# W_up loaded whole in pass 10 of the first loop, three chunks of W_down behind W_gate, and tile 1's attention result transposed by DMA

## The chip, the cores and the metric

The kernel runs on one core of a Trainium2 chip. A core has a matrix engine (TensorE, PE in the profile, with its weight loads as PEld), a vector engine (VectorE, DVE), an engine for activations (ScalarE, ACT), a general engine (GpSimd, POOL) and SyncE (SP), which here issues nearly all transfers. SBUF is the working memory, PSUM the accumulator memory that TensorE writes, with eight banks. The metric is the device time of one execution in microseconds; the median of three runs of the kernel before is 271.67 us, the lowest 271.39 and the highest 271.82.

## The reference

One transformer block on x of 2048 rows and 640 columns in bf16: linear attention with 32 heads of 20 columns, then a gated feed-forward part with 1536 hidden columns.

```python
def _A_ref(x, wqkv, w_phi, wo):
    qkv = (x @ wqkv).reshape(B, S, 3, H, Dh) ...     # q, k, v by head
    pq = einsum("bhsd,hdf->bhsf", q, w_phi)
    pk = einsum("bhsd,hdf->bhsf", k, w_phi)
    phi_q = concat([softmax(pq), softmax(-pq)])
    phi_k = concat([softmax(pk), softmax(-pk)])
    kv = einsum("bhsf,bhsd->bhfd", phi_k, v)
    z  = einsum("bhsf->bhf", phi_k)
    num = einsum("bhqf,bhfd->bhqd", phi_q, kv)
    den = einsum("bhqf,bhf->bhq", phi_q, z) + 1e-6
    return (num / den) ... @ wo

def _B_ref(x, w_gate, w_up, w_down):
    return (gelu(x @ w_gate) * (x @ w_up)) @ w_down

h = x + _A_ref(layernorm(x), wqkv, w_phi, wo)
out = h + _B_ref(layernorm(h), w_gate, w_up, w_down)
```

## The kernel before

The rows are cut into 16 tiles of 128 (t = 0 to 15) and four blocks of four tiles (b = 0 to 3). The order of all engines' work is written out by hand: the order of the calls is the order on each engine, and waits and slots follow from it.

**First part.** Weights of q and k are multiplied with w_phi in the kernel (`fold`, L232). The loop of L494 runs over the 16 tiles. Each pass makes k of one tile (`k_tile`, pk), normalizes its exponentials (`k_norm`), and v of a later tile (`v_mm`, pv); layer-normalized rows are transposed by DMA into LN1T (`ln_ap`, L286). In passes 7 to 10 the q weights are loaded transposed (`load_T`, L203). In pass 10 tile 1's rows are transposed into LN1T of block 0 (L529), in pass 13 those of tile 0 (L531). In pass 15 the first four groups of q columns are multiplied (`q_mm`, pq, L396), the second of them from block 0, and `kv_tile` sums the key-value products. Behind the first of these groups a copy on GpSimd into Wg (L513) holds back the load of W_gate; after the loop SyncE issues W_gate in two parts (L539) and two of five row chunks of W_up (L540).

**The stretch around the change (L856 to L912).** Here the remaining q groups alternate with the attention of tiles 0 and 1. For one tile t: `attn_a` multiplies phi_q with kv and z (ab) and copies it to SBUF; `attn_b`, `attn_b2`, `attn_b3` divide by the sums on VectorE and leave o (L687); then o is transposed into oT, by DMA (`transpose_to` at L167) or on TensorE with a copy by ScalarE (L164, L165); `attn_c` multiplies oT with W_o (po, L708) in two halves of 320 columns; `attn_d` adds the residual into x_sb (L717); `attn_ds` takes the statistics (L121, L125; the reciprocal root on GpSimd, L140); `attn_ln` normalizes (L156) and `attn_e` transposes by DMA into LN2T, which the gate and up matmuls read. For tile 0 the transpose of o is a DMA; for tile 1 it is done on TensorE, between the two halves of tile 0's `attn_c`. After tile 0's `attn_b3` SyncE issues the other three chunks of W_up (L555) and three of twelve chunks of W_down (L560); five more follow behind a copy on GpSimd (L907), the last four later.

Then `gate_first` and `gate_second` make the first gate and up products, of tile 0 and then of tile 1 (gu, L762), and `weave` interleaves the rest: gate and up of each block, the attention of the later tiles, and `down` (pd, L814), which reads W_down and stores the output.

**PSUM.** Up to this point, and until `split` (L567), PSUM is a pool of four slots of two banks each (`gtile`); pq, ab, po, tp and gu take them in turn, each waiting until the slot's last tile has been read. A slot number is not written in the code: it follows from the order in which slots come free. After `split` there are eight slots of one bank (`bank`).

Of the kernel before, what the change touches and what calls it, by code (L numbers as in the profile page):

```python
# [8 lines left out]
BF16 = mybir.dt.bfloat16  # L9
F32 = mybir.dt.float32  # L10
ALU = mybir.AluOpType
# [6 lines left out]
def kernel(  # L18
# [12 lines left out]
    nc = tc.nc  # L31
    P = 128
    S = 2048
    D = 640
# [5 lines left out]
    NC = D // P  # L40
    NF = FF // P
    EPS = 1e-5
    HD = D // 2

    H0 = [(P * c) // Dh for c in range(NC)]
    NH = [(P * c + P - 1) // Dh - H0[c] + 1 for c in range(NC)]
# [31 lines left out]
    const = ctx.enter_context(tc.tile_pool(name="const", bufs=1))  # L78
# [8 lines left out]
    Wo = const.tile([P, NC, D], BF16, name="Wo")  # L87
    Wg = const.tile([P, NC, FF], BF16, name="Wg")
    Wu = const.tile([P, NC, FF], BF16, name="Wu")
    KT = [const.tile([P, SL * 32], BF16, name=f"KT{s}") for s in range(2)]  # L90
    KV = [const.tile([P, SL, 32], BF16, name=f"KV{s}") for s in range(2)]
    row = const.tile([P, 3, 32], F32, name="row")
# [3 lines left out]
    Eq = [const.tile([P, len(g), 2, 512], BF16, name=f"Eq{j}") for j, g in enumerate(QG)]  # L96
# [14 lines left out]
    def gtile(name):  # L111
        return psG.tile([P, 2, 512], F32, name=name, tag="G")
# [46 lines left out]
    def transpose_to(dst, src, on_pe, on_dve=False):  # L159

        if on_pe:
            tp = psG.tile([P, 16, P], BF16, name="tp", tag="G")
            for c in range(NC):
                nc.tensor.transpose(tp[:, c, :], src[:, c * P:(c + 1) * P], ident)  # L164
            (nc.vector.tensor_copy if on_dve else nc.scalar.copy)(dst, tp[:, 0:NC, :])  # L165
        else:
            nc.sync.dma_start_transpose(dst, src)  # L167
# [326 lines left out]
    for t in range(NT):  # L494
        if t == T3:
            kvp = gtile("kvp")[:, 0, 0:2 * QF].rearrange("p (s f) -> p s f", s=2)
        late = t in (1, 2, 3, 4)
        if 0 < t < NT - 6 and not late:
            ln_ap(t + 6, on_act=True)
        k_tile(t)  # L500
        if t == 0:
            ln_ap(6)
            nc.sync.dma_start(x_sb[3][:, 0:2, :], x_v[:, 12:14, :])
        if t in FQ:
            fold(WqT, Wq2, True, [i for i, f in enumerate(FQ) if f == t])
# [12 lines left out]
        if late:  # L518
            ln_ap(t + 6, on_act=True)
        if t == 1:  # L520
            nc.sync.dma_start(x_sb[3][:, 2:4, :], x_v[:, 14:16, :])
        if 0 < t < NT - 3:
            v_ev(t + 3)
        for i in ST.get(t, ()):
            ln_st(i, i + 1)
        k_norm(t)
        load_T(WqT, 0, *[i for i, f in enumerate(LQ) if f == t])
        if t == 10:
            transpose_to(LN1T[0][:, :, P:2 * P], ln_a(1), False)  # L529
        if t == 13:  # L530
            ln_ap(0, on_act=True)  # L531
        if t == 8:
            for z in KT:
                nc.gpsimd.memset(z, 0.0)
        if t == 5:
            nc.sync.dma_start(Wo, wo_v)
    q = len(QT)
    for a, b in ((0, 2), (2, NC)):
        nc.sync.dma_start(Wg[:, a:b], wg_v[:, a:b])  # L539
    nc.sync.dma_start(Wu[:, 0:2], wu_v[:, 0:2])  # L540
    for t in range(13, NT):
        kv_tile(t)
    kv_mask()
# [3 lines left out]

    p2 = ctx.enter_context(tc.tile_pool(name="p2", bufs=1, reuse_waits="tile"))
    p2r = ctx.enter_context(tc.tile_pool(name="p2r", bufs=1, side="right", reuse_waits="tile"))
    Wd = p2r.tile([P, NF, D], BF16, name="Wd")  # L550
    wd_v = B_w_down.rearrange("(c p) n -> p c n", p=P)

    def load_up():

        nc.sync.dma_start(Wu[:, 2:NC], wu_v[:, 2:NC])  # L555

    def load_down(*fs):

        for f, n in fs:
            nc.sync.dma_start(Wd[:, f:f + n], wd_v[:, f:f + n])  # L560

    ABs = [p2r.tile([P, 2, H, KC], F32, name=f"AB{i}") for i in range(2)]
    ABs += [LN1F[:, i * 2 * H * KC:(i + 1) * 2 * H * KC].rearrange("p (s h f) -> p s h f", s=2, h=H) for i in range(2)]
    LN2T, st = {}, {}
# [114 lines left out]
    def attn_b3(t, on_pe=False):  # L679
        AB, w = st[t]  # L680
        tt = p2.tile([P, 2, D], BF16, name="tt", bufs=2)
        num = bass.AP(AB.tensor, AB.offset, [AB.ap[0], [H * KC + 1, 2], [KC, H], [1, Dh]])
        nc.vector.tensor_tensor(  # L683
            tt.rearrange("p s (h f) -> p s h f", f=Dh), num,
            w[:, :, :, None].to_broadcast([P, 2, H, Dh]), ALU.mult)
        o = p2.tile([P, D], BF16, name="o", bufs=2)
        nc.vector.tensor_tensor(o, tt[:, 0], tt[:, 1], ALU.add)  # L687
        st[t] = o
        if not on_pe:
            attn_t(t, False)  # L690

    def attn_t(t, on_pe=True):
        oT = p2.tile([P, NC, P], BF16, name="oT", bufs=3)
        transpose_to(oT, st[t], on_pe)
        st[t] = oT

    def attn_c(t, between=None):

        if psB:
            po = pos = [bank("po")[:, 0:HD] for u in range(2)]  # L700
        else:
            po = gtile("po")
            pos = [po[:, u, 0:HD] for u in range(2)]
        for u in range(2):
            if u and between:
                between()
            for c in range(NC):
                nc.tensor.matmul(pos[u], lhsT=st[t][:, c, :], rhs=Wo[:, c, u * HD:(u + 1) * HD],  # L708
                                 start=(c == 0), stop=(c == NC - 1))
        st[t] = po  # L710

    def attn_d(t, act=True):

        ht = x_sb[t // 4][:, t % 4, :]
        h2 = ht.rearrange("p (u f) -> p u f", u=2)
        if not act:
            nc.vector.tensor_tensor(h2, st[t][:, :, 0:HD], h2, ALU.add)  # L717
# [82 lines left out]
    def down(b, tl, u, cut, pair):  # L800

        if u == 0:
            st["y"] = p2.tile([P, D], BF16, name="y", bufs=4)
        y = st["y"]
        last = b == NB - 1 and tl == 3
        edges = [(0, cut), (cut, D)][u]
        if last and u == 1:
            edges = (cut, cut + 192, D)
        for f0, f1 in zip(edges, edges[1:]):
            pd, rest = bank("pd"), None  # L810
            for f in range(NF):
                if f == NF // 2 and pair is not None:
                    rest = attn_two(pair, pd)
                nc.tensor.matmul(pd[:, 0:f1 - f0], lhsT=st[b, "g", f][:, tl * P:(tl + 1) * P],  # L814
                                 rhs=Wd[:, f, f0:f1], start=(f == 0), stop=(f == NF - 1), skip_group_check=pair is not None)
            nc.vector.tensor_tensor(y[:, f0:f1], pd[:, 0:f1 - f0], x_sb[b][:, tl, f0:f1], ALU.add)  # L816
# [45 lines left out]
    attn_b(0, True)  # L862
    attn_b2(0, True)
    attn_b3(0)
    load_up()
    load_down((0, 3))
    attn_a(1, 0)
    q_exp(q + 1, (0,))
    q_mm(q + 2)
# [2 lines left out]
    q_mm(q + 3)  # L872
    attn_b(1, True)
    attn_b2(1, True)
    attn_b3(1, True)
    q_exp(q + 2, (1,))
    q_mm(q + 4, (0,), (0, 1))
    attn_c(0, lambda: attn_t(1))
    attn_d(0, False)
    q_exp(q + 3, (0,))  # L880
    q_mm(q + 4, (0,), (2, 3))
    attn_ds(0)
    attn_c(1)
    q_exp(q + 3, (1,))
    attn_d(1, False)
    q_mm(q + 4, (0,), (4,))
    q_mm(q + 4, (1,))
    q_exp(q + 4)

    def first():  # L890
# [1 line left out]
        attn_e(0, None)  # L892

    attn_ds(1, first)
    q_mm(q + 5)
    q_exp(q + 5)
    q_mm(q + 6)
    q_exp(q + 6)
# [8 lines left out]
    nc.gpsimd.tensor_copy(Wd[:, 3, 0:1], Eq[q + 8][:, 0, 1, 0:1])  # L907
    load_down((3, 5))
    attn_a(2, 2)
    for f in range(4):  # L910
# [56 lines left out]
```

## Time and profile before

The profiled execution took 271.45 us, with a span of 269.7 us from the first to the last instruction.

| | |
|---|---|
| median of three runs | 271.67 us |
| profiled execution, its span | 271.45 us, 269.7 us |
| VectorE busy | 173.4 us (64%) |
| ScalarE busy | 138.4 us (51%) |
| GpSimd busy | 101.4 us (38%) |
| mean DMA rate over the span | 83 GB/s |
| granted TensorE clock | 1.000 |

In the profile an arrow points from what is read to what is written (out<-in), L is a line of the kernel, and a time in brackets is idle time of the engine ahead of the row with what ended it. TensorE's matmuls overlap in its pipeline, so a matmul's recorded duration is longer than the distance to the next; the chain of work that ended last gives the distances. The start of a row in the chain is therefore a little later than the start of the same instruction in the timeline.

### The profile page before, as it was taken

How to read it: one execution, taken by the hardware profiler on the slowest of the kernel's cores; microseconds unless marked ns; L12 is line 12 of the kernel's file. 1: busy time of each engine (PE TensorE's matmuls, PEld its weight loads, DVE VectorE, ACT ScalarE, POOL GpSimd, SP SyncE). 2: the span in 40 equal slices, each digit the busy share in tenths (PEclk: the TensorE clock that was granted, in tenths of full speed). 3: DMA queues.
4: the chain of work that ended last, by engine and by line, in shares of the span. 5: the costliest groups of instructions: out<-in, count | busy, mean ns of one | idle time of the engine just before them, and what ended most of it. 6: DMA issues, size and time to landing. Idle time of an engine off the chain costs nothing.

```text
span 269.7 us, 7099 instructions
## 1 busy us (share of the span) xinstructions
PE 266.0 (99%) x2892; PEld 172.4 (64%) x2892; DVE 173.4 (64%) x346; ACT 138.4 (51%) x247; POOL 101.4 (38%) x239
## 2 busy tenths in 40 slices
PE   8999999999999999999999999999999999999995
PEld 7777777755456877788755555775555476444574
DVE  5899999995875858875566783568664322333322
ACT  5779997877789665245541456321544300322100
POOL 5448988796003235375211664014661100000000
PEclk9999999999999999999999999999999999999999
DMA  6996579214673443234201225203222101000011
GB/s 192 211 212 150 103 195 92 53 29 137 276 254 73 147 123 70 58 74 52 51 27 49 49 50 51 51 2 79 76 43 49 24 24 51 24 0 2 1 49 49
DMA packets 45952, 22.27 MB, mean 83 GB/s; under 512 B 38496, under 2 KB 43872, under 8 KB 45920
## 3 DMA queue, kind: packets, MB, share of 16 engines
q1 hardware_dynamic: 45264, 21.80, 33.9%
q8 instruction: 22, 0.36, 0.6%
q10 hardware_dynamic: 656, 0.03, 0.2%
q14 instruction: 10, 0.08, 0.1%
HBM read 10.18 MB, written 2.62 MB: 47 GB/s over the span
## 4 chain that ended last, share of the span: by engine, by line
PE 97%; DMA 2%; SPq 0%; DVE 0%; issue 0%
PE gu L762 39%; PE pd L814 20%; PE pq L396 8%; PE pk L296 8%; PE po L708 8%; PE pv L296 7%; PE kvp L374 2%; DMA Wv<-in_A_wqkv_dram 2%; PE pv L312 2%; PE ab L619 1%; PE wa L248 1%; PE ab L586 1%; PE tp L164 0%; SPq L193 0%; SPq L190 0%; SPq L189 0%
## 5 line engine op out<-in xcount | busy, mean ns | idle before, releaser
L795 ACT ACTIVATE g<-gu 128x512 bf16<-128x512 f32 (+1 forms) x56 | 28.9, 519 | 73.4 <-PE gu L762 73.3
L762 PE MATMUL gu<-LN2T,Wg 128*128 128x512 bf16 (+2 forms) x320 | 62.5, 326 | 0.0
L762 PE MATMUL gu<-LN2T,Wu 128*128 128x512 bf16 (+2 forms) x320 | 62.5, 326 | 0.0
L798 DVE TENSOR_TENSOR GT<-gu,g 128x512 bf16<-128x512 f32 (+1 forms) x56 | 32.7, 591 | 45.6 <-PE gu L762 38.8
L814 PE MATMUL pd<-Wd,GT 128*128 128x320 bf16 (+4 forms) x396 | 53.9, 296 | 0.0
L814 PEld LDWEIGHTS <-GT 128*128 128x128 bf16 x396 | 37.6, 98 | 14.5 <-DVE GT L798 0.2
L762 PEld LDWEIGHTS <-Wu 128*128 128x128 bf16 x320 | 30.0, 98 | 22.4
L762 PEld LDWEIGHTS <-Wg 128*128 128x128 bf16 x320 | 29.7, 98 | 21.1 <-issue 0.2
L296 PEld LDWEIGHTS <-LN1T 128*128 128x128 bf16 x290 | 27.9, 98 | 10.4
L355 POOL TENSOR_TENSOR E<-E,rs 128x640 bf16<-128x640 bf16 x25 | 31.7, 1296 | 4.4 <-DVE rs L351 1.7
L816 DVE TENSOR_TENSOR y<-pd,x_sb 128x320 bf16<-128x320 f32 (+4 forms) x33 | 15.8, 480 | 24.1 <-PE pd L814 24.1
L708 PE MATMUL po<-Wo,oT 128*128 128x320 bf16 x160 | 24.5, 299 | 0.0
L296 PE MATMUL pk<-Wk,LN1T 128*128 128x320 bf16 x160 | 24.4, 300 | 0.0
L347 DVE TENSOR_REDUCE sk<-E 128x64 f32<-128x1280 bf16 x16 | 22.9, 1431 | 0.0
L396 PE MATMUL pq<-LN1T,Wq 128*128 128x512 bf16 x100 | 22.8, 380 | 0.0
L401 ACT ACTIVATE Eq<-pq 128x1024 bf16<-128x1024 f32 (+1 forms) x26 | 19.9, 832 | 2.5 <-PE pq L396 2.4
L340 ACT ACTIVATE E<-pk 128x640 bf16<-128x640 f32 x28 | 19.0, 766 | 3.0 <-PE pk L296 3.0
L708 PEld LDWEIGHTS <-oT 128*128 128x128 bf16 x160 | 15.6, 98 | 7.3 <-ACT oT L165 0.2
L296 PE MATMUL pv<-Wv,LN1T 128*128 128x320 bf16 x130 | 19.8, 300 | 0.0
L151 ACT ACTIVATE ln<-x_sb,v,rstd 128x640 bf16<-128x640 bf16 x14 | 12.9, 920 | 13.0 <-POOL v L747 12.8
L396 PEld LDWEIGHTS <-Wq 128*128 128x128 bf16 x100 | 9.5, 98 | 10.5
L683 DVE TENSOR_TENSOR tt<-AB,w 128x1280 bf16<-128x1280 f32 x10 | 15.1, 1507 | 1.0 <-POOL w L676 0.9
(122 smaller groups left out, 292.8 us busy)
## 6 DMA issues: line engine op xcount, KB each, us to landing
out_dram<-y SPq DMA_DIRECT2D x15, 160.0 KB, 1.9
x_sb<-in_A_x_dram SPq DMA_DIRECT2D x6, 320.0 KB, 3.5
Wg<-in_B_w_gate_dram SPq DMA_DIRECT2D x1, 1152.0 KB, 6.7
Wu<-in_B_w_up_dram SPq DMA_DIRECT2D x1, 1152.0 KB, 5.7
Wo<-in_A_wo_dram SPq DMA_DIRECT2D x1, 800.0 KB, 5.1
Wd<-in_B_w_down_dram SPq DMA_DIRECT2D x1, 800.0 KB
Wg<-in_B_w_gate_dram SPq DMA_DIRECT2D x1, 768.0 KB
Wu<-in_B_w_up_dram SPq DMA_DIRECT2D x1, 768.0 KB, 7.8
```

Source lines behind the costliest of these rows:

```text
L296: nc.tensor.matmul(ps[:, u, 0:HD], lhsT=lnT(t, c), rhs=W[:, c, u * HD:(u + 1) * HD], start=(c == 0), stop=(c == NC - 1))
L340: nc.scalar.activation(Ek[t][:, s, :].rearrange("p (u f) -> p u f", u=2), pk[:, :, 0:HD], ACTF.Exp, scale=((lnp[t][2], nrstd[t]) if t in C ...
L347: nc.vector.reduce_sum(sk, Ek[t].rearrange("p s (h f) -> p (s h) f", f=Dh), axis=AX.X)
L355: eng.tensor_tensor(e, e, rs[:, s * H:(s + 1) * H, None].to_broadcast([P, H, Dh]), ALU.mult)
L396: nc.tensor.matmul(pqs[j][:, i, :], lhsT=Wq2[:, kc, c * P:(c + 1) * P], rhs=LN1T[b][:, kc, :], start=(kc == 0), stop=(kc == NC - 1))
L401: nc.scalar.activation(Eq[j][:, :, s, :], pqs[j][:, 0:len(QG[j])], ACTF.Exp, scale=(1.0, -1.0)[s])
L708: nc.tensor.matmul(pos[u], lhsT=st[t][:, c, :], rhs=Wo[:, c, u * HD:(u + 1) * HD], start=(c == 0), stop=(c == NC - 1))
L762: nc.tensor.matmul(gu[i][:, 0:a1 - a0], lhsT=W[:, c, f * P:(f + 1) * P], rhs=LN2T[b][:, c, a0:a1], start=(c == 0), stop=(c == NC - 1))
L795: nc.scalar.activation(g[:, 0:n], gu[0][:, 0:n], ACTF.Gelu_apprx_tanh)
L798: nc.vector.tensor_tensor(st[b, "g", f][:, a0:a1], gu[1][:, 0:n], g[:, 0:n], ALU.mult)
L814: nc.tensor.matmul(pd[:, 0:f1 - f0], lhsT=st[b, "g", f][:, tl * P:(tl + 1) * P], rhs=Wd[:, f, f0:f1], start=(f == 0), stop=(f == NF - 1), ...
L816: nc.vector.tensor_tensor(y[:, f0:f1], pd[:, 0:f1 - f0], x_sb[b][:, tl, f0:f1], ALU.add)
```

## The change

W_up is loaded in one transfer of 1920 KB, issued by SyncE in pass 10 of the loop, behind the last part of the q weights and ahead of tile 1's transpose. Behind W_gate the first three chunks of W_down (480 KB) take the place of the two chunks of W_up; they have a tile of their own, Wd0, and the other nine chunks are in Wd1. The loads after tile 0's `attn_b3` are gone.

Tile 1's o is transposed by DMA like tile 0's. On TensorE the order becomes: both halves of tile 0's `attn_c`, the last three of five matmuls of q group 8, the first three of q group 9, `attn_c` of tile 1, the other two of group 9. Tile 1's residual is added in two halves of 320 columns. A tile of one slot of PSUM is taken by a memset of one element on VectorE, between tile 1's residual and its statistics.

```diff
+    ND = 3
+    Wd0 = const.tile([P, ND, D], BF16, name="Wd0")
...
         if t == 10:
+            nc.sync.dma_start(Wu, wu_v)
             transpose_to(LN1T[0][:, :, P:2 * P], ln_a(1), False)
...
     for a, b in ((0, 2), (2, NC)):
         nc.sync.dma_start(Wg[:, a:b], wg_v[:, a:b])
-    nc.sync.dma_start(Wu[:, 0:2], wu_v[:, 0:2])
+    nc.sync.dma_start(Wd0, wd_v[:, 0:ND])
...
-    Wd = p2r.tile([P, NF, D], BF16, name="Wd")
+    Wd1 = p2r.tile([P, NF - ND, D], BF16, name="Wd1")
...
         if not act:
-            nc.vector.tensor_tensor(h2, st[t][:, :, 0:HD], h2, ALU.add)
+            for u in ((slice(0, 2),) if t == 0 else (slice(0, 1), slice(1, 2))):
+                nc.vector.tensor_tensor(h2[:, u], st[t][:, u, 0:HD], h2[:, u], ALU.add)
...
     attn_b3(0)
-    load_up()
-    load_down((0, 3))
     attn_a(1, 0)
...
-    attn_b3(1, True)
+    attn_b3(1)
     q_exp(q + 2, (1,))
     q_mm(q + 4, (0,), (0, 1))
-    attn_c(0, lambda: attn_t(1))
+    attn_c(0)
     attn_d(0, False)
     q_exp(q + 3, (0,))
-    q_mm(q + 4, (0,), (2, 3))
+    q_mm(q + 4, (0,), (2, 3, 4))
+    q_mm(q + 5, kcs=(0, 1, 2))
     attn_ds(0)
     attn_c(1)
     q_exp(q + 3, (1,))
     attn_d(1, False)
-    q_mm(q + 4, (0,), (4,))
-    q_mm(q + 4, (1,))
+    nc.vector.memset(gtile("skip")[0:1, 0, 0:1], 0.0)
     q_exp(q + 4)
...
     attn_ds(1, first)
-    q_mm(q + 5)
+    q_mm(q + 5, kcs=(3, 4))
     q_exp(q + 5)
```

More of the change, by code (lines that the diff above doesn't have):

```diff
@@ L537 @@
     q = len(QT)
+    wd_v = B_w_down.rearrange("(c p) n -> p c n", p=P)
     for a, b in ((0, 2), (2, NC)):
         nc.sync.dma_start(Wg[:, a:b], wg_v[:, a:b])
-    nc.sync.dma_start(Wu[:, 0:2], wu_v[:, 0:2])
+    nc.sync.dma_start(Wd0, wd_v[:, 0:ND])
     for t in range(13, NT):
@@ L549 @@
     p2r = ctx.enter_context(tc.tile_pool(name="p2r", bufs=1, side="right", reuse_waits="tile"))
-    Wd = p2r.tile([P, NF, D], BF16, name="Wd")
-    wd_v = B_w_down.rearrange("(c p) n -> p c n", p=P)
-    def load_up():
-        nc.sync.dma_start(Wu[:, 2:NC], wu_v[:, 2:NC])
+    Wd1 = p2r.tile([P, NF - ND, D], BF16, name="Wd1")
     def load_down(*fs):
         for f, n in fs:
-            nc.sync.dma_start(Wd[:, f:f + n], wd_v[:, f:f + n])
+            nc.sync.dma_start(Wd1[:, f - ND:f - ND + n], wd_v[:, f:f + n])
     ABs = [p2r.tile([P, 2, H, KC], F32, name=f"AB{i}") for i in range(2)]
@@ L814, in down @@
                 nc.tensor.matmul(pd[:, 0:f1 - f0], lhsT=st[b, "g", f][:, tl * P:(tl + 1) * P],
-                                 rhs=Wd[:, f, f0:f1], start=(f == 0), stop=(f == NF - 1), skip_group_check=pair is not None)
+                                 rhs=(Wd0[:, f, f0:f1] if f < ND else Wd1[:, f - ND, f0:f1]), start=(f == 0), stop=(f == NF - 1), skip_group_check=pair is not None)
             nc.vector.tensor_tensor(y[:, f0:f1], pd[:, 0:f1 - f0], x_sb[b][:, tl, f0:f1], ALU.add)
@@ L906 @@
     nc.scalar.add_instruction(mybir.InstLoadActFuncSet(name=nc.get_next_instruction_name(), act_func_set_id=11))
-    nc.gpsimd.tensor_copy(Wd[:, 3, 0:1], Eq[q + 8][:, 0, 1, 0:1])
+    nc.gpsimd.tensor_copy(Wd1[:, 0, 0:1], Eq[q + 8][:, 0, 1, 0:1])
     load_down((3, 5))
```

## The prediction

> **What bounds the kernel now.** I read the page first, its busy shares and its summary of the chain that ended last; then that chain in order of time; then the timeline of all engines around the edited lines, the SyncE queue's own timeline, and the views of single tiles for how long transfers take to land. The page, engine shares and chain by engine:
>
> ```profile
> span 269.7 us, 7099 instructions
> ...
> PE 266.0 (99%) x2892; PEld 172.4 (64%) x2892; DVE 173.4 (64%) x346; ACT 138.4 (51%) x247; POOL 101.4 (38%) x239
> ...
> PE 97%; DMA 2%; SPq 0%; DVE 0%; issue 0%
> ```
>
> TensorE is busy in 266.0 of 269.7 us and 97% of the chain lies on it. The profiled execution took 271.45 us, so 1.75 us lie around the span; it is 0.22 us (0.08%) below the median of the three runs, 271.67. The same chain in order of time, columns start, length, what, with the number of matmuls:
>
> ```profile
> 62.60 3.34 PE pq L396 x15
> ...
> 72.14 4.87 PE pq L396 x22
> 77.01 0.68 PE po L708 x5
> 77.69 0.28 PE tp L164 x5
> 77.97 0.68 PE po L708 x5
> 78.65 0.43 PE pq L396 x2
> 79.08 1.36 PE po L708 x10
> 80.44 4.53 PE pq L396 x21
> 84.97 0.40 PE ab L586 x39
> 85.37 2.90 PE gu L762 x50
> ...
> 103.06 2.46 PE pd L814 x18
> ```
>
> The reader is to see that each piece begins where the one before ended, and that their lengths are pure matmul streaming: 21 pq matmuls in 4.53 us are 0.216 each, ten po in 1.36 are 0.136 each. TensorE doesn't wait anywhere from 72 to 88 us, so this stretch can only get shorter by the matmuls taken out, and longer by any wait the new order makes. Who feeds it, from the timeline of all engines in that stretch (start, length, engine, line):
>
> ```profile
> 76.45 0.49 DVE L687 TENSOR_TENSOR o<-tt 128x640 bf16<-128x640 bf16 x1
> ...
> 78.01 0.69 ACT L165 COPY oT<-tp 128x640 bf16<-128x640 bf16 x1 [0.72 <-PE tp L164]
> ...
> 78.69 0.83 DVE L717 TENSOR_TENSOR x_sb<-po,x_sb 128x640 bf16<-128x640 f32 x1 [1.74 <-PE po L708]
> 78.75 1.35 PEld L708 LDWEIGHTS <-oT 128*128 128x128 bf16 x10 [0.16 <-ACT oT L165]
> ...
> 79.55 0.89 DVE L121 BATCH_NORM_STATS2 stats<-x_sb 128x6 f32<-128x320 bf16 x2
> ...
> 80.47 0.21 DVE L125 BATCH_NORM_AGGREGATE mv<-stats 128x2 f32<-128x12 f32 x1
> 80.60 0.77 DVE L717 TENSOR_TENSOR x_sb<-po,x_sb 128x640 bf16<-128x640 f32 x1
> ...
> 81.16 0.58 POOL L140 TENSOR_TENSOR rstd<-ve,nhalf 128x1 f32<-128x1 f32 x1
> 81.40 0.49 DVE L121 BATCH_NORM_STATS2 stats<-x_sb 128x6 f32<-128x320 bf16 x1
> 81.81 0.43 DVE L156 TENSOR_SCALAR ln<-x_sb,mv,rstd 128x640 bf16<-128x640 bf16 x1
> ...
> 85.31 0.45 PE L762 MATMUL gu<-LN2T,Wg 128*128 128x128 bf16 x5
> ```
>
> And the SyncE queue, which issues every load and every transpose by DMA in order:
>
> ```profile
> 42.85 4.47 SPq L203 DMA_TRANSPOSE WqT<-in_A_wqkv_dram  x3
> 51.46 4.63 SPq L167 DMA_TRANSPOSE LN1T<-ln  x2
> ...
> 63.55 1.19 SPq L539 DMA_DIRECT2D Wg<-in_B_w_gate_dram  x2
> ...
> 73.80 1.20 SPq L167 DMA_TRANSPOSE oT<-o  x1
> 75.05 0.58 SPq L555 DMA_DIRECT2D Wu<-in_B_w_up_dram  x1
> 75.80 0.37 SPq L560 DMA_DIRECT2D Wd<-in_B_w_down_dram  x1
> 82.27 3.30 SPq L167 DMA_TRANSPOSE LN2T<-ln  x2
> ```
>
> **The change part by part.**
>
> *Five transposes leave TensorE.* In the chain they are one piece, 77.69, of 0.28 us between two halves of po, whose 0.68 + 0.68 is what ten po cost elsewhere (1.36). So the gain is 0.28 us, and it is the only gain that the chain offers: -0.28. The row of the tile itself:
>
> ```profile
> L164 PE MATMUL tp<-ident,o x5: 219/219/220, 77.5 to 77.8; 128*128 128x128 bf16 x5
> ```
>
> The recorded duration of one is 219 ns, four times its share of the chain, because they overlap in the pipeline. [...] The chain's 0.28 for all five decides for the sum; a full price is a rival below.
>
> With them goes ScalarE's copy of 0.69 us at 78.01. ScalarE is not on the chain; its exponentials for the next pq come earlier, which is worth nothing while no matmul waits for a slot.
>
> *The transpose of tile 1 by DMA (term 2).* The vector add that makes o of tile 1 ends at 76.45 + 0.49 = 76.94. SyncE issues a transpose 0.03 after its input is there (ln ends 81.81 + 0.43 = 82.24, issue 82.27). Landing, for all seven oT transposes after 70 us:
>
> ```profile
> DMA to landing us min/median/max: 2.4/2.4/3.3
> ```
>
> With 2.4 (the least, and the median) oT lands at 76.97 + 2.4 = 79.37. TensorE now does attn_c(0), 1.36 from 77.01, three pq of group 8 and three of group 9, 6 x 0.216 = 1.29, and is there at 79.66. Before, the weight load was released at 78.01 + 0.69 = 78.70 and the matmuls ran on at 79.08 without a gap, 0.38 later; by that 79.37 gives 79.75. So the wait is 0 to 0.09 at this landing and 0.94 at the worst one (3.3). That one had a bulk load in front of it; here the queue is empty, because the loads at 75.05 and 75.80 leave this place. I take +0.05. Everything behind it on TensorE waits too, and attn_c(1) then runs 79.71 to 81.07, 0.63 later than before, since six pq matmuls now stand ahead of it and only two did.
>
> *The residual in halves, the memset, and LN2T of tile 0 (term 3).* VectorE's order is: residual 0, statistics 0, residual 1 in two adds, memset, first statistics of tile 1, then ln of tile 0, which feeds the first gate matmuls. The residual of tile 0 starts 0.04 after its matmuls (78.65, 78.69), now 78.41, and its rstd follows by the old distances at about 81.46 (78.69 to 81.16 + 0.58), so POOL isn't last. Last is the second half add, which needs all of attn_c(1): 81.07 + 0.04 = 81.11. Its price is that of the nearest shape, an add of 128x320 from PSUM:
>
> ```profile
> L816 DVE TENSOR_TENSOR y<-pd,x_sb 128x320 bf16<-128x320 f32 (+4 forms) x33 | 15.8, 480 | 24.1 <-PE pd L814 24.1
> ```
>
> So it ends at 81.59; two halves cost 0.96 against 0.77 to 0.83 for the whole, but the first lies under matmuls. The memset writes one element and no row shows one; it lies between nothing and the 0.21 of the small aggregate at 80.47. I take 0.10, since one element is nearer to nothing. Then 81.69, statistics until ln starts 0.41 (81.40 to 81.81), ln and issue 0.46: 82.56, against 82.27 before. Landing of the seven LN2T transposes:
>
> ```profile
> DMA to landing us min/median/max: 2.6/2.6/4.1
> ```
>
> So LN2T is there at 85.16 (before: 84.87, used at 85.31). TensorE after 81.07: two pq of group 9, fifteen of groups 10 to 12, 17 x 0.216 = 3.67, ab 0.40: the gate piece is due at 85.14, its first matmul 0.06 earlier as in the rows 85.31 and 85.37. That is a wait of 0.08; between 0 (cheap memset) and 0.3 (memset 0.21, one more step of the queue). I take +0.08. Tile 1 follows 2.10 later as before (issues at 82.27 and 82.27 + 3.30 - 1.20 = 84.37): landed 87.26, needed after 40 gate matmuls of 0.058 (2.90 for 50) at 87.54. Cover 0.28, cost nothing; if that is gone, each tenth late is a tenth of time.
>
> *PSUM slots.* po of tile 1 now takes a slot that the residual of tile 0 frees (78.41 + 0.83 = 79.24, needed 79.66): nothing. The memset's tile shifts the order: group 10 may get the slot of group 8 (free when its exponentials are done, ahead of 81) or that of po 1, free at 81.59 against 81.50 needed. Between 0 and 0.15, and not on top of term 3: what TensorE loses there it doesn't wait for at LN2T. I take 0.
>
> *The loads.* W_up whole, 1920 KB, is issued in pass 10 behind W_q's last transpose (42.85 + 4.47 = 47.32) and ahead of the two transposes at 51.46 and 54.89 of LN1T. The two W_gate loads have the same 1920 KB; the second's landing:
>
> ```profile
> DMA to landing us min/median/max: 6.7/6.7/6.7
> ```
>
> That is 63.55 to about 70.7, 7.2 us, so W_up is in at about 54.5. The DMA engines have room (0.24 share in this window):
>
> ```profile
> 47.00:55.00 8.00, 8.00 (x216) 6.23 (x214) 7.90 (x9) 6.78 (x11) 5.79 (x7) 1.00 0.24 47
> ```
>
> If the two LN1T transposes wait for the whole of it (the 3.3 among the oT landings shows that a transpose behind a load comes late), they land at 57 to 60; their reader is the pq piece at 62.60. Nothing waits, with 2.6 us to spare; SyncE itself stands idle from 47.32 to 51.46, which covers an issue of about 1.2 (both W_gate issues). [...] Behind W_gate, 480 KB of W_down replace 768 KB of W_up: the queue is empty before the oT issue at 73.80. Wd0 and Wd1 hold the same chunks, first read at 103.06: nothing.
>
> **Sum.** -0.28 + 0.05 + 0.08 = -0.15: 271.45 becomes 271.30, and on the median 271.67 becomes 271.5. A measurement here tells about 0.2% (0.54 us) from no change, so the forecast is the same time.
>
> **The rivals.**
> - Full gain: both waits vanish under weight loads that are released earlier. For it: both are under 0.1 us and within what the rows resolve. 271.67 - 0.28 = 271.4.
> - Late transpose (slower): oT of tile 1 lands like the 3.3 row, because its queue still moves something. 0.94 + 0.08 - 0.28 = +0.74: 272.4. It decides for slower once the wait passes 0.74, a landing over 3.1 us. For it: there is no cover beyond the six pq matmuls. Against it: no load is in the queue then.
> - A PSUM slot turned the wrong way: the first pd, 12 matmuls from 103.06, gets a slot that the last gate product holds. That product:
>
> ```profile
> 103.59 0.75 DVE L798 TENSOR_TENSOR GT<-gu,g 128x256 bf16<-128x256 f32 x2
> ```
>
> It ends at 104.34, so TensorE would stand 1.28 there: 271.5 + 1.3 = 272.8. For it: the order of slots changes and the profile shows no slot numbers; against it: with 97% of the chain on TensorE no slot costs anything now.
> - W_up in pass 10 delays LN1T past 62.60: LN1T would have to land 2.6 us later than I count; by the slowest transpose (4.1) behind a load that ends at 56, no. If it did by another 1.5, 273.
> - The transposes cost their full 219 ns: 5 x 0.219 = 1.10, 270.7 with the waits. Against it: the chain. [...]
>
> **How the numbers follow.** Forecast 0.48, full gain 0.27, wrong slot 0.11, late transpose 0.08, W_up 0.03, full transposes 0.03. Faster by over 0.2% (below 271.13): the last, and a quarter of the full gain by spread of the runs, 0.03 + 0.07 = 0.10. Slower (above 272.21): 0.11 + 0.08 + 0.03 = 0.22. Same: 0.68. The range reaches from the full gain less the spread of the medians (271.4 less the 0.43 between the lowest and the highest run) to the late transpose (272.4); left out are wrong slot, W_up and full transposes, 0.17.
>
> **What would show it.** In the new profile: no tp piece; the second po piece starts at 79.7 or so with a weight load that waits on a DMA; the first gate piece starts 0.1 to 0.2 before 85.37, after a wait on LN2T of under 0.3; from there every piece as long as before; the pq piece at 62.60 unmoved. Wrong would be any TensorE wait over 0.3 us, above all at 79.7, 85.2 or 103, or a gap-free chain that is shorter by more than 0.28.

## The result, and the profile after

The changed kernel takes 273.6 us (median of six runs, 272.81 to 274.09), the kernel before on the same chip 271.57: a ratio of 1.007, 95% interval 1.0052 to 1.0088. It is slower by 2.0 us, 0.7%; the forecast was 271.5, the same time. The profiled execution took 273.71 us, its span is 272.0 (before 269.7).

First the page of the changed kernel: span, TensorE's share, and the chain by engine.

```profile
span 272.0 us, 7073 instructions
...
PE 265.2 (98%) x2871; PEld 171.8 (63%) x2887; DVE 173.6 (64%) x348; ACT 137.6 (51%) x246; POOL 101.5 (37%) x239
...
PE 91%; DVE 4%; DMA 3%; issue 1%; DVEq 0%; SPq 0%
```

TensorE's share of the chain fell from 97% to 91%; VectorE, the DMA and "issue" (time in which the engine waits for nothing that the profile shows) took it. Where, says the view of TensorE's waits (line, what it waited for, us in total, times, longest):

```profile
PE po L707 <- DMA oT<-o: 1.3, 1, 1.3
PE wu L230 <- PEq L949: 0.8, 1, 0.8
PE kvp L376 <- issue: 0.6, 1, 0.6
PE gu L762 <- DMA LN2T<-ln: 0.4, 1, 0.4
```

The second row is the start of the kernel, in the profile of before too. The other three are new. The chain in order of time shows each at its place (start, length, what):

```profile
61.50 1.06 PE kvp L376 x119
62.56 0.65 issue
63.21 0.24 PE kvp L376 x9
63.45 0.32 PE pq L398
...
77.85 3.88 DMA oT<-o
...
81.78 1.54 PE po L707 x10
...
83.35 0.89 DVE x_sb L717 x2
...
85.03 2.58 DMA LN2T<-ln
...
87.74 2.95 PE gu L762 x50
...
105.34 2.46 PE pd L814 x18
```

Set against the rows of before: kvp with its stop lasts from 61.50 to 63.45, 1.95 us; before it lasted from 61.47 to 62.60, 1.13. That is +0.82, with 0.03 ahead of it. The second po starts at 81.78 instead of 80.5, where TensorE ran out of work, +1.26, and its ten matmuls take 1.54 instead of 1.36, +0.18. The wait on LN2T is 0.36. The five transposes are gone, -0.28. Together 0.03 + 0.82 + 1.26 + 0.18 + 0.36 - 0.28 = 2.37, and the first gate piece starts at 87.74 instead of 85.37: 2.37 later. The pd piece, at 105.34 instead of 103.06, is 2.46 long in both; no slot of PSUM was waited for.

VectorE's timeline at the third wait, from the end of the po piece at 83.32:

```profile
83.35 0.89 DVE L717 TENSOR_TENSOR x_sb<-po,x_sb 128x320 bf16<-128x320 f32 x2 [2.10 <-PE po L707]
...
84.23 0.06 DVE L885 MEMSET skip<- 1x1 f32 x1
84.56 0.43 DVE L158 TENSOR_SCALAR ln<-x_sb,mv,rstd 128x640 bf16<-128x640 bf16 x1
```

Both half adds stand in one row, 0.89 us from 83.35, behind the last of the ten po matmuls; the memset is 0.06.

What the DMA engines did, in two views. Between 47 and 55 us (columns: window, length, busy time and count of PE, PEld, VectorE, ScalarE, GpSimd, then clock, DMA share, GB/s):

```profile
47.00:55.00 8.00, 8.00 (x216) 6.21 (x215) 7.90 (x9) 6.81 (x11) 5.79 (x7) 1.00 0.84 259
```

The DMA share is 0.84 where it was 0.24. W_up, issued at 47.96, landed at 56.3 and not at 54.5 (the page's list of issues: KB, us to landing):

```profile
Wu<-in_B_w_up_dram SPq DMA_DIRECT2D x1, 1920.0 KB, 8.4
```

The last view is the DMA traffic while oT of tile 1 is on its way (40 slices of 0.14 us from 76.5; then the queue of instructions, its packets, MB and share of 16 engines; then the transpose and its us from issue to landing):

```profile
GB/s 12 0 0 0 0 0 0 0 0 0 0 0 0 0 0 0 0 0 69 259 287 292 361 42 0 0 0 0 0 0 2 0 0 0 0 0 0 0 0 0
...
q8 instruction: 1, 0.02, 1.1%
...
oT<-o SPq DMA_TRANSPOSE x1, 3.9
```

The transpose landed 3.9 us after its issue at 77.85, not 2.4. Its packets run from 78.9 to 79.8, and one slice at 80.7 still moves something; in the same window one packet of 16 KB was read by another queue, named "instruction". It went from 79.65 to 80.66: the late slice comes right behind it, and oT landed 1.1 us after its end (77.85 + 3.88 = 81.73).

### The profile page after: what moved, and what is told of

It is laid out like the page before. It is cut to its first block, busy times and chain, and to the rows that moved or that the text cites. A ratio compares the mean times of both kernels' runs of the same rounds, so it can differ in the third digit from the quotient of the medians.

```text
span 272.0 us, 7073 instructions
## 1 busy us (share of the span) xinstructions
PE 265.2 (98%) x2871; PEld 171.8 (63%) x2887; DVE 173.6 (64%) x348; ACT 137.6 (51%) x246; POOL 101.5 (37%) x239
## 4 chain that ended last, share of the span: by engine, by line
PE 91%; DVE 4%; DMA 3%; issue 1%; DVEq 0%; SPq 0%
PE gu L762 38%; PE pd L814 19%; PE pk L298 8%; PE po L707 8%; PE pv L298 7%; PE pq L398 4%; PE kvp L376 2%; PE pv L314 2%; DMA oT<-o 1%; PE ab L618 1%; PE wa L250 1%; DVE tt L682 1%; DMA LN2T<-ln 1%; DMA x_sb<-in_A_x_dram 1%; PE tp L166 1%
## 5 line engine op out<-in xcount | busy, mean ns | idle before, releaser
L342 ACT ACTIVATE E<-pk 128x640 bf16<-128x640 f32 x28 | 18.4, 724 | 3.0 <-PE pk L298 3.0
```

Source lines behind the costliest of these rows:

```text
L342: nc.scalar.activation(Ek[t][:, s, :].rearrange("p (u f) -> p u f", u=2), pk[:, :, 0:HD], ACTF.Exp, scale=((lnp[t][2], nrstd[t]) if t in C ...
```

## The experiments

The theory with which they began: the three waits have three causes. One, the packets of 16 KB of the queue named "instruction" are blocks of TensorE's instructions, and W_up, 1920 KB, puts them back. The page counts 22 of them, on the same 16 DMA engines as the loads; for 2887 pairs of weight load and matmul that is 131 pairs to a packet, which I took for 128 (an estimate: no view says whose instructions they are). Two, such a block on its way holds up oT of tile 1. Three, the halves of the residual don't overlap with po. The rival to each is said with its run. Each run was compared with the kernel before on the same chip; a profile shows one execution, which can lie off the median.

**Loads alone.**

```diff
-    attn_b3(1)
-    attn_c(0)
+    attn_b3(1, True)
+    attn_c(0, lambda: attn_t(1))
...
```

The residual is whole again and the pq matmuls stand as before (not shown); the loads are those of the change.

> Loads as in the changed kernel (W_up whole in pass 10, Wd0 behind W_gate), TensorE's order, the five transposes and the whole residual as before. Theory: W_up fills the DMA engines from 48 to 56 us, TensorE's next block of instructions (queue q8, 16 KB) is fetched 2.4 us late, and TensorE stands 0.65 us inside the key-value products at 62.5; so this kernel is slower than the one before by 0.6 to 0.9 us (about 272.4) with that same gap. Rival: the loads are innocent and the whole loss hangs on the new transpose; then 271.6, with no gap at 62.5.

Measured: 272.38 us against 271.71, ratio 1.003 (1.0012 to 1.0047). The time is the theory's, but the profiled execution, 271.88 us, is quicker than that median and has no stop in kvp. The early load costs 0.7 us in the median, and this run doesn't show where.

**One chunk of W_up.** Only the first of five chunks is loaded and read for all five, so the up product isn't the reference's.

```diff
-            nc.sync.dma_start(Wu, wu_v)
+            nc.sync.dma_start(Wu[:, 0:1], wu_v[:, 0:1])
```

> The changed kernel, but only the first of five chunks of W_up is loaded in pass 10 (384 KB), and every up matmul reads that chunk; so the up product isn't the reference's, the work on every engine is the same. Theory: without the long load the instruction fetch is on time and the 0.65 us gap at 62.5 is gone, while oT of tile 1 still lands 3.9 us after its issue because the fetch of the next block falls on it: 273.6 - 0.85 = 272.7. Rival (the gap has nothing to do with W_up's bytes): 273.6 and the gap stays.

Measured: 273.07 us, ratio 1.0051 (1.0037 to 1.0065). No stop in kvp in its profile (272.19 us, the quickest of its five runs); oT of tile 1 still came late (landing 3.1), po began 0.5 us late for it, and the wait on LN2T was 0.35. By the profile the early load is a part of the loss, not the whole; by the time alone that isn't shown, since this interval overlaps that of the changed kernel.

**Twelve more pairs in the warm-up**, in the changed kernel and in the one-chunk kernel (whose up product isn't the reference's either), to move the borders between blocks.

```diff
-    warm(*[512] * 2, *[P] * 28)
+    warm(*[512] * 2, *[P] * 24, *[32] * 16)
```

> The changed kernel with 12 more weight load and matmul pairs in the warm-up at the start (24 of 128 columns and 16 of 32 instead of 28 of 128), so that every border between instruction blocks comes 12 pairs earlier in the work. Theory: the fetch that fell on tile 1's oT (79.65 to 80.66) then ends before that transpose moves its data; oT lands 2.4 to 2.6 us after its issue and TensorE waits for it under 0.3 us instead of 1.3: 273.6 - 1.3 = 272.3, with the gap in the key-value products still there. Rival (this transpose is slow by itself, for instance because another went just ahead of it): landing 3.9 and 273.6.

> Both of the last two edits: one chunk of W_up loaded and read for all five (the up product isn't the reference's), and 12 more pairs in the warm-up. Theory: both losses gone, what is left is the change as I had summed it, -0.15 to -0.28 against the kernel before: 271.3 to 271.5. Rival (a third cause, for instance a slot of PSUM or LN2T): over 271.8.

Measured: 274.65 us, ratio 1.0098 (1.0079 to 1.0117), and 272.76, ratio 1.0039 (1.0023 to 1.0055). Both missed. In both profiles oT of tile 1 now landed in 2.4 us; but oT of tile 0 was late instead (landings 3.1 and 3.3; in the second kernel a block's packet went 0.7 us behind its issue), and in the first TensorE ran dry at another place, for 1.2 us at 57.47. The weight loads of that kernel:

```profile
56.02 1.25 PEld L298 LDWEIGHTS <-LN1T 128*128 128x128 bf16 x10
58.67 1.31 PEld L398 LDWEIGHTS <-Wq 128*128 128x128 bf16 x7 [1.41 <-issue]
```

The stop has the same mark as the one in kvp: no wait on a semaphore, and it comes behind the 734th weight load of the kernel (the 722nd in the changed kernel's trace, and twelve more), where the changed kernel stopped behind the 861st: 127 apart, one block of 128 to within one. The second kernel lies 1.3 us over my expectation. Its profiled run, 274.32 us, is far above its median. Besides its waits (1.2 at the start on W_v, 0.2 at po, 0.3 at LN2T) its mean granted clock is 0.994; 0.006 of its span of 272.4 us is 1.6 (an estimate), and without it the run would stand at about 272.7, near the median. It is the only one of its eleven runs with a mean clock under 0.999. What the others waited for isn't profiled.

**po of tile 1 in two PSUM tiles.**

```diff
             pos = [po[:, u, 0:HD] for u in range(2)]
+            if t == 1:
+                pos[1] = gtile("po")[:, 1, 0:HD]
...
-    nc.vector.memset(gtile("skip")[0:1, 0, 0:1], 0.0)
```

> The changed kernel with one more edit: the two halves of po of tile 1 get a PSUM tile each (the second takes the slot that the one-element memset held), the memset is gone. Theory (the first half add waits for all ten po matmuls because both halves lie in one PSUM tile): now the first half add runs under the second five matmuls, ln of tile 0 starts about 0.4 us sooner behind po, and the wait of the first gate matmul on LN2T, 0.36 us in the changed kernel, is under 0.1: 273.3 us against 273.6. Rival (the wait comes from the landing of LN2T, not from the halves): the wait stays over 0.3 us and the time at 273.6. The wait of po on oT (1.3 us) and the stop in kvp (0.65 us) stay by either.

Measured: 273.3 us against 271.34, ratio 1.0062 (1.0038 to 1.0086). The time is as expected, but it doesn't decide between theory and rival: its runs lie between 271.43 and 273.94. The profile does: the wait on LN2T is gone, the other two are there, 1.3 and 0.3. VectorE's timeline now has the half adds as two rows:

```profile
82.55 0.49 DVE L720 TENSOR_TENSOR x_sb<-po,x_sb 128x320 bf16<-128x320 f32 x1 [1.46 <-PE po L710]
83.23 0.49 DVE L720 TENSOR_TENSOR x_sb<-po,x_sb 128x320 bf16<-128x320 f32 x1 [0.19 <-PE po L710]
```

The first starts at 82.55, 0.68 ahead of the second, while TensorE makes the second half. So this loss was in the shared tile: in the changed kernel the add that reads one half of it waited for the last matmul into the other.

**W_up split.** Three chunks in pass 10, two behind W_gate, W_down's first three behind LN2T.

```diff
-            nc.sync.dma_start(Wu, wu_v)
+            nc.sync.dma_start(Wu[:, 0:3], wu_v[:, 0:3])
...
-    nc.sync.dma_start(Wd0, wd_v[:, 0:ND])
+    nc.sync.dma_start(Wu[:, 3:NC], wu_v[:, 3:NC])
...
+    nc.sync.dma_start(Wd0, wd_v[:, 0:ND])
     load_down((3, 5))
```

> The changed kernel with its loads laid out anew: three chunks of W_up (1152 KB) in loop pass 10, the other two (768 KB) behind W_gate, the first three chunks of W_down behind LN2T of tile 1. Theory (TensorE's instruction blocks come late behind 1920 KB): the load is in by about 53, the block of 54.1 comes on time, TensorE doesn't stop in kvp: 272.9 to 273.1 us. The wait on oT of tile 1 (0.5 to 1.3 us) and that on LN2T (0.36 us) stay. Rival (the loads have no part in it): 273.6.

Measured: 273.25 us, ratio 1.0073 (1.006 to 1.0086). The stop in kvp is gone, as the theory has it, but the time hardly moved. The weight loads near 95 us show where the gain went:

```profile
94.92 0.10 PEld L762 LDWEIGHTS <-Wu 128*128 128x128 bf16 x1
95.51 0.42 PEld L762 LDWEIGHTS <-Wu 128*128 128x128 bf16 x4 [0.50 <-issue]
```

The 480 + 800 KB of W_down are now issued together, behind LN2T of tile 1 (86.2) and ahead of the block of 93.0, and TensorE stopped for 0.32 us behind its 1372nd weight load (by the order in the changed kernel's trace): 511 on from the 861st, four blocks of 128 to within one. The next run, with the same loads, stops there too; no kernel without them does. The wait at po (1.3) and that on LN2T (0.3) were there too, and 0.4 and 0.6 ahead of 7 us, on the first tiles; waits there come and go between executions.

**Split, two PSUM tiles, and two more pq matmuls ahead of po.**

```diff
-    q_mm(q + 5, kcs=(0, 1, 2))
+    q_mm(q + 5)
...
-    q_mm(q + 5, kcs=(3, 4))
```

> The changed kernel with three edits: the loads as in the split (three chunks of W_up in pass 10, two behind W_gate, W_down behind LN2T), po of tile 1 in two PSUM tiles without the memset, and all five pq matmuls of group 9's step ahead of po of tile 1 (0.43 us more cover for oT). Theory (three separate losses: instruction blocks behind the load 0.65, oT late by a block's packet 0.5 to 1.3, halves that don't overlap 0.36): the stop in kvp and the LN2T wait are gone, the po wait is 0 to 0.8 by the landing of oT: 271.5 to 272.2 us, 271.8 in the middle. Rival (the losses have one cause that stays, so that one wait takes the place of another): 272.7 or more.

Measured: 273.14 us, ratio 1.0059 (1.0042 to 1.0076), against an expected 271.8. Its waits:

```profile
PE po L710 <- DMA oT<-o: 1.2, 1, 1.2
...
PE gu L765 <- DMA LN2T<-ln: 0.4, 1, 0.4
PE gu L765 <- issue: 0.3, 1, 0.3
```

The cover of 0.43 bought 0.1: here oT landed 4.3 us after its issue, the block's packet being at 79.2. LN2T, which hangs behind this po, was late again by 0.4: the two matmuls moved ahead of po are no longer behind it to cover LN2T. The last row is the stop of the split. The rival said that one wait would take another's place, and in this run it did.

**Three chunks of W_gate early as well**, on the order of before.

```diff
             transpose_to(LN1T[0][:, :, P:2 * P], ln_a(1), False)
+            nc.sync.dma_start(Wg[:, 2:NC], wg_v[:, 2:NC])
```

> The kernel before, attention as before, with W_up whole in pass 10 and besides three chunks of W_gate (1152 KB) right behind the two LN1T transposes of that pass: the suspected cause made larger. Theory (blocks of instructions queue behind bulk loads): the next blocks (58.6 and 63.3 us in the kernel before) come some 2 us late or more, and TensorE stops with no wait on a semaphore for 1.5 to 3 us between 58 and 68: 273.5 to 275 us. Rival (the early load costs something else, or nothing): 272.4 as with W_up alone, no such stop.

Measured: 273.63 us in the median of all nine runs (272.49 to 277.93), 273.01 in that of the seven from which the ratio, 1.0091 (1.0059 to 1.0124), is taken. The first is just in the range, the second isn't, and the mechanism wasn't mine:

```profile
PE pq L398 <- DMA LN1T<-ln: 3.1, 1, 3.1
```

TensorE waited 3.1 us, at 59.26, for the transposes of LN1T, which landed 7.2 to 7.5 us after their issues. The same pq piece, at 57.16 in the kernel before, is where the changed kernel reads them: it has 20 matmuls, groups 0 and 1, and group 1 is the one that needs tile 1. The profiled run took 276.11 us, 2.5 over the median, with a granted clock of 0.50 for 3.4 us behind this wait; how long the quicker runs waited isn't shown.

**W_up spread out, with two PSUM tiles.** Three chunks ahead of the LN1T transposes of pass 10, one behind them, one behind W_gate, then W_down as in the change.

```diff
-            nc.sync.dma_start(Wu, wu_v)
+            nc.sync.dma_start(Wu[:, 0:3], wu_v[:, 0:3])
             transpose_to(LN1T[0][:, :, P:2 * P], ln_a(1), False)
+            nc.sync.dma_start(Wu[:, 3:4], wu_v[:, 3:4])
...
+    nc.sync.dma_start(Wu[:, 4:NC], wu_v[:, 4:NC])
     nc.sync.dma_start(Wd0, wd_v[:, 0:ND])
```

> The changed kernel with two edits: W_up spread out (three chunks, 1152 KB, in pass 10 ahead of the LN1T transposes, one behind them, the last behind W_gate, then the first three chunks of W_down), and po of tile 1 in two PSUM tiles without the memset. Theory: no stop in kvp, no wait on LN2T; po waits 1.2 to 1.3 us for oT of tile 1, because a block of instructions is fetched between 78.5 and 79.7, while oT is on its way, and the last packets of oT come behind it: 1.0 us over the kernel before (-0.28 for the five transposes, +1.25 for this wait), 272.5. Rival (the stop in kvp or the LN2T wait comes back in another place): 273 or more.

Measured: 272.65 us against 271.44, ratio 1.0047 (1.0035 to 1.006): as expected. Behind 7 us the only wait left is the one at po:

```profile
PE po L712 <- DMA oT<-o: 1.4, 1, 1.4
...
PE pv L314 <- DMA Wv<-in_A_wqkv_dram: 0.4, 1, 0.4
```

**The same with twenty warm-up matmuls, and the kernel before with them.**

```diff
-    warm(*[512] * 2, *[P] * 28)
+    warm(*[512] * 5, 256, *[P] * 14)
```

> The same with one more edit: the warm-up on TensorE has 20 matmuls instead of 30 (five of 512 columns, one of 256, fourteen of 128; about the same columns in all), so that each border between blocks of 128 pairs of weight load and matmul lies ten pairs later in the kernel's work. Theory (what makes oT late is the block fetched while it is on its way): the fetch comes at 80 or later, behind oT, which lands 2.4 us after its issue; po waits under 0.2 us, and the kernel takes 0.1 to 0.3 us less than the kernel before, 271.2 to 271.5. Rival (oT of tile 1 is late for another reason, such as its place in the queue or its own shape): the wait stays at 1.2 and the time at 272.5.

> Control: the kernel before with the shorter warm-up alone. Theory (it only moves the borders of the blocks; in the kernel before no transpose that TensorE waits for is on its way at a border): the time of the kernel before, 271.3 to 271.7. Rival (the warm-up has a price or a gain of its own, so that the comparison of the two others tells nothing of oT): off by more than 0.4 us.

Measured: 273.89 us, ratio 1.0088 (1.0072 to 1.0103), and 271.96, ratio 1.0019 (1.001 to 1.0028). Both missed; the second by the control's rival, off by more than 0.4 us. The block came at 79.2, still inside the way of oT (issued 77.41), and po waited 1.3: the shift was too small. The warm-up has a price of its own, 0.5 us. Why the first took 1.2 us more than the spread kernel, where its profile shows the same wait, stays open beyond these 0.5.

**The attention order alone**, with the loads of before.

```diff
-            nc.sync.dma_start(Wu, wu_v)
...
+    nc.sync.dma_start(Wu[:, 2:NC], wu_v[:, 2:NC])
+    nc.sync.dma_start(Wd0, wd_v[:, 0:ND])
     attn_a(1, 0)
```

> One part alone: the attention order, the oT by DMA, the halves and the memset of the changed kernel, with the loads of the kernel before (two chunks of W_up behind W_gate, three more and three of W_down, 1632 KB, issued at about 75, just ahead of oT of tile 1). Theory (oT queues behind the bulk load): the load holds the DMA engines from 75 to about 81, oT lands at 81.5 to 83, and po waits 2 to 3.5 us; no stop in kvp: 274 to 275. Rival (early W_up is the whole of the loss, the attention order costs nothing): 271.3.

Measured: 278.14 us, ratio 1.0246 (1.0232 to 1.026): the theory's sign, twice its size. The wait, the chain behind it, and one window of the busy times (the granted clock is the third column from the end):

```profile
PE po L706 <- DMA oT<-o: 4.9, 1, 4.9
```

```profile
76.82 7.52 DMA oT<-o
...
84.39 2.85 PE po L706 x10
87.24 4.34 PE pq L398 x17
```

```profile
84.00:86.00 2.00, 1.61 (x7) 0.93 (x8) 0.00 (x0) 0.00 (x0) 0.00 (x0) 0.50 0.00 0
```

oT landed 7.52 us after its issue, behind 1632 KB, so po waited 4.9 us instead of 2 to 3.5. In that wait the granted clock fell to 0.50, and it stayed there until 88.5 (0.88 in the mean from 88 to 90): ten po matmuls took 2.85 us for 1.36, the next 17 pq and their like 4.34 for 3.67, another 2.2 us. So the move of W_up wasn't idle: without it the transpose by DMA at this place makes the kernel 6.7 us slower.

**Ten warm-up matmuls, in the spread kernel and in the kernel before.** It moves the block of 79 further back than twenty did.

```diff
-    warm(*[512] * 2, *[P] * 28)
+    warm(*[512] * 8, *[P] * 2)
```

> The spread loads and the two PSUM tiles for po of tile 1, now with ten warm-up matmuls instead of 30 (eight of 512 columns, two of 128). With twenty the block came at 79.2, still inside the way of oT of tile 1 (77.0 to 81), so that the shift had been too small by some 0.8 us of work; ten more pairs are 1.4 to 2.1 us. Theory (a block fetched while oT is on its way makes it late): the border now lies behind the first weight load that needs oT of tile 1, so no block is fetched between 77 and 80; oT lands 2.4 us after its issue and po waits under 0.2 us, and against the kernel before with the same warm-up the time is 0.0 to 0.3 us less. Rival (oT of tile 1 is late whatever the block does): it lands 3.9 or later, po waits 1.2, 1.0 us more than that kernel.

> Control: the kernel before with the warm-up of ten matmuls. With twenty it took 0.5 us more than the kernel before and showed a wait of 1.0 us on W_v at the start. Theory (the warm-up changes the start, by the same amount in both): 271.5 to 272.5 us, with the waits before 10 us holding all that is over 271.5. Rival (the moved borders bring a stop of their own later): a stop of over 0.3 us behind 40 us.

Measured: 271.47 us against 271.39, ratio 1.0001 (0.999 to 1.0012), and 271.91, ratio 1.0015 (1.0007 to 1.0023). The wait at po is gone, as the theory has it. The weight loads of the first, then its chain:

```profile
79.48 1.27 PEld L712 LDWEIGHTS <-oT 128*128 128x128 bf16 x10 [0.24 <-DMA oT<-o]
```

```profile
62.67 3.34 PE pq L398 x15
...
78.44 1.29 PE pq L398 x6
79.73 1.36 PE po L712 x10
...
85.16 2.90 PE gu L767 x50
```

The transpose was issued at 77.07; the weight load that needs it goes at 79.48, so oT took 2.4 us. It waits 0.24 itself, the matmuls run on without a gap, and the block's packet comes at 80.4, when oT is there. From the first row of the chain to the gate piece it is 85.16 - 62.67 = 22.49 us; in the kernel before 85.37 - 62.60 = 22.77. The difference is 0.28, the five transposes. In the medians it is 271.91 - 271.47 = 0.44 under the kernel before with the same warm-up, more than the 0.0 to 0.3 expected; the two intervals overlap a little. The control's profile, 271.34 us, is its quickest run and doesn't show where its median lost 0.5 us.

**As long a warm-up as before, still ten matmuls** (the diff is against the run before this one).

```diff
-    warm(*[512] * 8, *[P] * 2)
+    warm(*[512] * 9, P)
```

> The version without the three waits (spread loads, two PSUM tiles for po of tile 1, ten warm-up matmuls), with the warm-up as long as before: nine matmuls of 512 columns and one of 128, 4.0 us instead of 3.8. If the 0.5 us that the shorter warm-up cost the kernel before came from its earlier end, this takes 0.1 to 0.4 us less than the kernel before, 271.0 to 271.3. If that price lies elsewhere (the load of W_v at the start comes when it comes), it stays level with the kernel before, 271.4 to 271.6.

Measured: 271.47 us against 271.38, ratio 1.0004 (0.9995 to 1.0013). This is the second reading of the expectation: the price isn't in the warm-up's length, as far as one kernel shows it; the kernel before wasn't run with this warm-up. The profile has a wait of 0.5 on W_v at the start and no other beyond 0.2; where the warm-up's 0.5 us come from isn't settled, and no version here beats the kernel before.

## Why the prediction was wrong

**"I take +0.05" for oT of tile 1 (term 2): 1.44.** This is the largest miss. Working from a landing of 2.4 because "here the queue is empty", I looked at the bulk loads alone. The packets of the queue named "instruction" go over the DMA engines too. But for the run with a load ahead of it, the recorded landings of the two transposes of oT in this stretch, in the changed order, are 2.4 us (nine) or 3.1 to 4.3 (eight). In the views that show these packets one goes on the way of each late transpose (six of the eight), and none on the way of the others (four of the nine). The ten-matmul warm-up moved the packet and the landing fell to 2.4, with the wait. The first weight load of this po stands close to a border itself (the 1120th; 861 + 2 x 128 = 1117), but it was oT that it waited for: in the changed kernel it goes at 81.77, 0.04 us after the landing. In the kernel before the same block came at 81.2, behind the loads of 75, and the next transpose, LN2T, issued at 82.27 as the packet ended (82.34), landed in its usual 2.6 us. The rival "late transpose" had the right place and the right sign, with 0.94 for the wait and 0.08 as its chance; its cause (a load in the queue) was not the one.

The row behind that rival was misread: the transpose with the landing of 3.3 was issued at 95.26 and the load of W_down beside it at 96.52, so the load was not in front of it. What held it up isn't settled; a packet of 8 KB of a second queue named "instruction" fell on its way, at 97.0. And the sign of the true cause stood in the profile of before, in the landing of 4.1 among the LN2T transposes, issued at 100.95. DMA traffic from 100.9, in 40 slices of 0.11 us:

```profile
GB/s 0 0 0 0 0 0 0 0 0 0 0 105 207 214 214 223 207 205 254 10 0 0 0 0 0 0 0 0 0 0 0 0 0 0 0 74 0 0 0 0
...
q8 instruction: 1, 0.02, 1.5%
...
LN2T<-ln SPq DMA_TRANSPOSE x1, 4.1
```

No load is under way there. A block's packet went from 102.9 to 104.0, and LN2T landed at 105.1, 1.1 us after it, as oT of tile 1 does above. The rest of this trace and that of the changed kernel agree. Of their oT and LN2T transposes after 60 us with a recorded landing, those on whose way no packet of 8 or 16 KB of either queue named "instruction" fell landed in 2.37 to 2.45 us (oT, 20 of them) and 2.56 to 2.63 (LN2T, 19). All eight in which a packet of 16 KB began 0.86 to 2.04 us behind the issue landed in 3.47 to 4.29, 1.0 to 1.6 us after the packet's end. One that had ended 0.8 us after the issue did no harm (four cases, 2.37 to 2.58).

**"Nothing waits, with 2.6 us to spare" for the loads: 0.82.** Two things failed. LN1T of tile 1 is read in the pq piece at 57.16, not at 62.60; no wait came of that in the changed kernel, though the transposes landed 4.0 and 6.5 us after their issues, but 3.1 us came of it in the profile with W_gate early as well. And what the load did put back were the blocks of instructions. DMA traffic of the kernel before from 57.5 and of the changed one from 60, in 40 slices of 0.06 us, each with a single packet:

```profile
GB/s 0 0 0 0 0 0 0 0 0 0 0 0 0 0 0 0 0 262 0 0 0 0 0 0 0 0 0 0 0 0 0 0 0 0 0 0 0 0 0 0
...
q8 instruction: 1, 0.02, 3.1%
```

```profile
GB/s 0 0 0 0 0 262 0 0 0 0 0 0 0 0 0 0 0 0 0 0 0 0 0 0 0 0 0 0 0 0 0 0 0 0 0 0 0 0 0 0
...
q8 instruction: 1, 0.02, 3.6%
```

The block came at 58.6 before and at 60.35 now, and its packet took 1.2 and 1.45 us (the share, times 16 engines, times 2.5 us). The weight loads of the changed kernel at the stop:

```profile
61.43 1.03 PEld L376 LDWEIGHTS <-vS 128*32 128x32 bf16 x119 [0.42 <-issue]
63.20 0.14 PEld L376 LDWEIGHTS <-vS 128*32 128x32 bf16 x9 [0.74 <-issue]
```

119 of kvp's 128 went, then nothing for 0.74 us, then nine. There are five stops of this kind in the profiles, behind weight loads 734, 861 (two kernels) and 1372 (two kernels), whole blocks of 128 apart to within two. In the four whose packet a view shows, TensorE went on 1.3 to 1.4 us after the packet had landed; here 60.35 + 1.45 + 1.4 = 63.2. How large this loss is depends on the execution: 0.65 in one profile, 0.3 in another, none in that of the loads alone. kvp runs through 128 pairs in 1.1 us, and the block ahead of this one had come at 56.48, right behind the landing of W_up at 56.33, where it came at 54.12 before. That W_up held both blocks back is my reading of these times; no view shows what a packet of this queue waits for.

**+0.08 for LN2T of tile 0 (term 3): 0.36.** My working let the first half add lie under the matmuls. It waits for all ten, as the timeline showed and two PSUM tiles undid: the two adds end 0.92 us after po and not 0.52. The memset, put at 0.10, is 0.06.

**Right:** the gain of the five transposes is 0.28 by the chain, not the 1.1 us of five recorded durations. The PSUM slots cost nothing; the pd piece at 105.34 has its old length. Wd0 and Wd1 cost nothing. With the three waits gone po started at 79.73 and the gate piece at 85.16, where the forecast had 79.7 and 85.14. The schedule was counted well; what was missing was a user of the DMA engines that made TensorE wait nowhere in the kernel before. Not explained are the 0.7 us that the early loads cost in the median of the run with the loads alone, whose profile has none of the three waits, the price of the warm-up, and the excess of the runs with the moved borders named above.

## What to carry to other kernels

Before a load or a transpose by DMA is moved, look at the blocks of instructions: find the 16 KB packets of the queue named "instruction" in the profile, and put bulk loads and transposes on the critical path where none falls. A transpose for which 2.4 us of cover were enough took 3.1 to 4.3 us here where one began in the 2.2 us behind its issue. Where 128 short matmuls follow each other in about a microsecond, as in kvp, a long load ahead of the block behind them can cost a stop (here 0.3 and 0.65 us in two profiles, none in a third). Two halves of a result overlapped here with what reads them only in PSUM tiles of their own (the first add then began 0.68 us ahead of the second).

## What the runs showed of the hardware

The 22 packets of 16 KB of the queue named "instruction" took 0.88 to 1.54 us each in the kernel before and in the changed one; an oT on whose way one fell landed 0.7 to 1.9 us later than its 2.4. In four profiles TensorE, having stopped with no wait on a semaphore, went on 1.3 to 1.4 us after such a packet had ended.

TensorE's clock held through the wait of 1.3 us in the changed kernel (granted 1.00 throughout). In the wait of 4.9 us it fell to 0.50 at 81.6, 2.2 us after TensorE had run dry, and the slow matmuls behind the wait brought another 2.2 us. In the profile with W_gate early it was 0.50 from 63.2 to 66.6, behind the wait of 3.1 us. It lasted 3.4 us there, and 6.8 behind the wait of 4.9. The profile of the one-chunk kernel with twelve more pairs, with a longest wait of 1.2 us, has a mean clock of 0.994; that of W_up spread out, with one of 1.4, has 1.00 from 0 to 110 us. So how long a wait is enough isn't settled.
